# Two experts instead of one get a first part of 256 slots, ahead of the last routing

## The chip, the cores and the metric

The kernel runs on one core of one Trainium2 chip. The metric is device time in microseconds (us) for one launch. In the text PE is the engine for matrix products (TensorE), DVE is VectorE, ACT is ScalarE, POOL is GpSimd, and SP is SyncE, which here only issues transfers. Each of these engines works through a list of its own, in the order of that list. "PEld" is the load of the stationary operand into PE's array.

## The reference, cut to what matters

Three stages follow each other. The first is an attention whose mask lets a query see a key only if both fall in the same of 64 buckets; the second is a dense layer pair with a gated activation; the third is a mixture of eight experts, of which each token takes the best two.

```python
# stage 1: 2 batches, 8 heads, 768 positions, 64 wide
scores = np.where(q_bucket == k_bucket, scale * q @ k.T, -1e9)
x = softmax(scores) @ v                        # -> 1536 tokens x 512
# stage 2
h = x @ w_in                                   # 512 x 2048
x = (h * sigmoid(1.702 * h)) @ w_out           # 2048 x 512
# stage 3: 8 experts, 512 -> 1024 -> 512
noisy = x @ w_gate + log1p(exp(x @ w_noise)) * noise
top2, weights = two largest of noisy per token, softmax over the two
for e in range(8):
    out[mask_e] += weight_e * (relu(x[mask_e] @ w1[e]) @ w2[e])
```

## The kernel before, in words

All products are done in float16 pairs: a value is split into a high and a low half, and three products (high by high, high by low, low by high) stand for one. This goes for the weights too: `w12_split` makes the two halves of a block of expert weights (128x1024), the high one on ACT (L742), the low one on DVE (L743). An expert has eight such blocks, four of w1 and four of w2. They are loaded by `w12_load` on SP into `w32`, of which there are four buffers (`w` in the trace's names), and split into `ew` tiles in the pool `wts`, which has four buffers: two hold one expert's w1 and w2, the other two the next one's. Before the experts the same four hold the weights of stage 2 (`wi` and `wo`).

The 1536 tokens go through stages 1 and 2 in six chunks of 256. A chunk's stage 2 ends with the products `px` (L471), whose two halves of 128 tokens are written to `xr` by ACT (L485) and DVE (L494) and transposed by a DMA to `xrt` (`r_t`). Then `route` works out the two experts of each token. It is written as a generator: products with the gate weights (`pz`, L578 and L580) on PE, a copy on ACT (`zc`, L583), a long run of small operations on DVE with three exponentials on ACT between them (L586 to L645), a count of the tokens ahead of each on PE (`pp`, L650), and a last run on DVE (L655 to L679) that ends with the slot numbers `si`. Four indirect transfers by POOL (L685) then write the chunk's rows to `slots` in DRAM, each to its expert's region of 400 slots.

The experts come after the last chunk. A list `seq` is the order of the steps on PE: a step is either one of the eight slices of an expert's first layer (`l1`, 12 products of the slots' transposed rows `xg` with `ew`, into one of three `ph` tiles in PSUM; ACT, L809, and DVE, L810, empty it into `ht` one step later) or one of the tiles of 128 slots of its second layer (`l2`, `py`), whose result `l2_out` scales on ACT and adds to the output with an indirect transfer by POOL. `e_load` transposes an expert's slots from DRAM to `xg` (L756) and fetches their token numbers and weights (`mt`); `e_meta` makes the scale from these on DVE (L776 to L786).

The last chunk's routing would leave PE idle. So expert 0 is cut in two parts: `reserve` moves its counter up after chunk 4 has been routed, so that the last chunk's tokens stand in slot 256 and above, and slots 0 to 255, the part (0, 0), can be worked on while the last chunk is routed. The part (0, 1) has the other 144 slots. How many experts are cut is `EA`, here 1; the other seven have one part of 400. The last routing is taken apart as `QX` pieces for each step of `seq`.

From step 100 of the program's main loop on, the lists of the engines are as the code emits them. The code is arranged by step numbers: `at(g, f)` puts f behind the rest of step g, `start` and `soon` put it further ahead in it.

```python
w32: x = m2.tile([128, 1024], F32, name="w32", bufs=4)
l1:  ph = psum2.tile([128, CAP], F32, name="ph", bufs=3)
pool of ew, wi, wo: wts = ctx.enter_context(tc.tile_pool(name="wts", bufs=4))
```

Of the kernel before, what the change touches and what calls it, by code (L numbers as in the profile page):

```python
# [52 lines left out]
SW2 = 2.0 ** 6  # L53


PARAM = dict(GM=16, HE=lambda nm, b: 'D', OE=lambda nm, b: 'D', SC=lambda nm, b: 'D', WB=0, XO=lambda b: 'D', NG=16, WS=lambda i: 'P', TS=lambda g: True, XL=lambda g: 'D', GW=2, E0=7, T0=12, T1=16, EL=8, WX=3, PV={(1,2,3):4}, PVD=5, ST={}, VA={}, RA={}, O0=48, OS=2, IS=2, FU=16, VF=2, EC=lambda g: 'AA', QX=8, QS=3, EA=1, S1=(8,8,8,9,9,9,11,13), QE=8, XG=2, XB=2, PC=2, OH=3, BK=3, R0=18, R1=0, LK=8, WL=1, NW=3, LE=lambda nc: nc.scalar, I0=24, LQ=8, LV=0, W=[(g, 1) for g in range(-6, 30)], KA={(0,0,0):-8,(0,0,1):-6,(0,1,0):-4,(0,1,1):-2}, QA={(0,0,0):-7,(0,0,1):-3}, HI=lambda g: 'P', LO=lambda g: False)
# [1095 lines left out]
```

## Time and profile before

| | |
|---|---|
| median of 3 runs | 826.06 us (823.59 to 827.4) |
| the profiled execution | 823.72 us, its span 822.0 us, the rest before its first and after its last instruction |
| PE busy | 715.9 us, 87% of the span |
| DVE busy | 533.9 us, 65% |
| ACT busy | 445.0 us, 54% |
| POOL busy | 267.9 us, 33% |
| DMA | 140.04 MB, mean 170 GB/s |

The span counts from the first to the last instruction. An engine's busy share is an average over the three stages. The experts start some 522 us after the span's start and take the rest of it; PE is busy there with two exceptions.

### The profile page before, as it was taken

To read this page: it belongs to the slowest core of one execution; us is meant where nothing else is said; L and a number is where in the kernel's file an instruction comes from. 1 tells how busy PE (TensorE), PEld (TensorE's weight loads), DVE (VectorE), ACT (ScalarE), POOL (GpSimd) and SP (SyncE) were. 2 spreads that over 40 slices of the span, in tenths; PEclk is the share of its full clock that TensorE was granted. 3 is DMA by queue.
4 is the path that set the end of the run, shared out by engine and by line. 5 is a ranking of instruction groups with operands and counts; after the bars stand their busy time and mean duration, and the time that the engine had idled before them with its cause. 6 is when DMAs were issued, how large, how long until landed. Compare 5 with 4: busy or idle time off the path is not lost.

```text
span 822.0 us, 14816 instructions
## 1 busy us (share of the span) xinstructions
PE 715.9 (87%) x5398; PEld 446.0 (54%) x5399; DVE 533.9 (65%) x1330; ACT 445.0 (54%) x859; POOL 267.9 (33%) x303
## 2 busy tenths in 40 slices
PE   1676478988988888898999999879999999999995
PEld 1343345646754665466568576547554655556553
DVE  8998799997896789569869526454633525345210
ACT  3778767766765686467567425234533534334220
POOL 6444646560444055314212132241021120311212
PEclk9878789999999999999999999999999999999998
DMA  8999689999999999995797542856875858677213
GB/s 218 224 251 212 180 187 184 255 277 218 175 171 195 154 200 192 225 159 106 119 176 123 102 156 88 221 146 180 250 158 173 199 111 232 135 194 176 28 19 47
DMA packets 268126, 140.04 MB, mean 170 GB/s; under 512 B 224720, under 2 KB 243856, under 8 KB 268048
## 3 DMA queue, kind: packets, MB, share of 16 engines
q1 hardware_dynamic: 261520, 125.37, 68.1%
q0 software_dynamic: 6528, 13.68, 9.3%
q8 instruction: 43, 0.70, 0.4%
q14 instruction: 35, 0.29, 0.1%
HBM read 61.48 MB, written 23.79 MB: 104 GB/s over the span
## 4 chain that ended last, share of the span: by engine, by line
PE 42%; DVE 5%; DMA 3%; POOL 2%; issue 1%; ACT 1%; POOLq 0%; ACTq 0%; DVEq 0%
PE ph L799 15%; PE py L821 13%; PE px L471 6%; PE h L460 3%; PE py L825 2%; DVE er L323 1%; DMA xg<-slots 1%; PE pv L368 1%; POOL slots L685 1%; DMA slots<-xr,si 1%; DMA et<-er 1%; PE s L254 1%; ACT er L314 1%; DVE e L266 1%; DVE th L490 1%
## 5 line engine op out<-in xcount | busy, mean ns | idle before, releaser
L460 PE MATMUL h<-xt,wi 128*128 128x256 f16 x1152 | 140.2, 277 | 6.2 <-DVE mx L279 3.2
L799 PE MATMUL ph<-xg,ew 128*128 128x400 f16 (+2 forms) x864 | 135.4, 320 | 8.9 <-DMA xg<-slots 8.4
L743 DVE SCALAR_TENSOR_TENSOR ew<-w,ew 128x1024 f16<-128x1024 f32 x64 | 77.9, 1226 | 88.2 <-ACT ew L742 88.0
L471 PE MATMUL px<-wo,gt 128*128 128x512 f16 x576 | 132.6, 382 | 0.5 <-DVE th L490 0.4
L460 PEld LDWEIGHTS <-wi 128*128 128x128 f16 x1152 | 112.5, 99 | 28.2 <-issue 9.1
L821 PE MATMUL py<-ew,ht 128*128 128x512 f16 x576 | 125.8, 379 | 0.0
L838 POOL DMA_INDIRECT out_dram<-yo,ti x32 | 51.2, 1600 | 216.7 <-ACT yo L835 216.7
L254 PE MATMUL s<-kt,qt 128*128 128x512 f16 (+1 forms) x384 | 88.2, 353 | 33.3 <-DVE mx L266 28.5
L799 PEld LDWEIGHTS <-ew 128*128 128x128 f16 x864 | 82.6, 100 | 59.8 <-issue 6.8
L275 ACT ACTIVATE e<-e,mx 128x768 f32<-128x768 f32 x96 | 89.4, 931 | 27.9 <-DVE mx L266 21.5
L505 POOL TENSOR_TENSOR gt<-th,gt 128x512 f16<-128x512 f32 x48 | 60.1, 1252 | 122.0 <-ACT gt L504 121.6
L266 DVE CUSTOM_DVE_ANT_0 e<-s,zero 128x768 f32<-128x768 f32 x96 | 90.6, 948 | 4.4 <-PE s L254 1.5
L821 PEld LDWEIGHTS <-ht 128*128 128x128 f16 x576 | 56.3, 98 | 67.0
L471 PEld LDWEIGHTS <-gt 128*128 128x128 f16 x576 | 55.3, 98 | 64.1 <-issue 3.2
L323 DVE SCALAR_TENSOR_TENSOR er<-e,mx,er 128x768 f16<-128x768 f32 x68 | 73.1, 1080 | 25.9 <-ACT er L314 25.3
L314 ACT ACTIVATE er<-e,mx 128x768 f16<-128x768 f32 x68 | 63.0, 930 | 37.8 <-DMA et<-er 21.6
L835 ACT ACTIVATE yo<-py,wv 128x512 f32<-128x512 f32 (+1 forms) x32 | 20.3, 633 | 102.4 <-PE py L821 54.6
L809 ACT ACTIVATE ht<-ph 128x400 f16<-128x400 f32 (+2 forms) x72 | 33.5, 466 | 73.0 <-PE ph L799 72.9
L254 PEld LDWEIGHTS <-qt 128*128 128x128 f16 x384 | 37.0, 103 | 62.7 <-issue 38.5
L810 DVE SCALAR_TENSOR_TENSOR ht<-ph,ht 128x400 f16<-128x400 f32 (+2 forms) x72 | 37.6, 524 | 49.5 <-ACT ht L809 49.5
L742 ACT ACTIVATE ew<-w 128x1024 f16<-128x1024 f32 x64 | 66.3, 1047 | 2.6 <-DMA w<-in_moe_w_dram 2.6
L368 PE MATMUL pv<-et,vt 128*64 128x256 f16 x720 | 51.2, 284 | 7.5 <-DMA et<-er 7.5
(195 smaller groups left out, 945.8 us busy)
## 6 DMA issues: line engine op xcount, KB each, us to landing
w<-in_moe_w_dram SPq DMA_DIRECT2D x64, 512.0 KB, 4.6
wraw<-in_moe_w_in_dram SPq DMA_DIRECT2D x16, 512.0 KB, 4.6
wraw<-in_moe_w_out_dram SPq DMA_DIRECT2D x16, 512.0 KB, 4.3
slots<-blank SPq DMA_DIRECT2D x6, 1032.0 KB, 6.8
v<-in_v_dram SPq DMA_DIRECT2D x24, 192.0 KB, 4.1
out_dram<-zeros SPq DMA_DIRECT2D x13, 256.0 KB, 3.4
k<-in_k_dram SPq DMA_DIRECT2D x16, 192.0 KB, 3.6
q<-in_q_dram SPq DMA_DIRECT2D x24, 128.0 KB, 3.1
```

The costliest lines, as they stand in the source:

```text
L254: nc.tensor.matmul(ps[:, n0 * 128:n1 * 128], qt[:, s, h, t, :], kt[:, s, h, n0:n1, :].rearrange("p c t -> p (c t)"), start=(s == 0), stop= ...
L266: nc.vector.tensor_tensor_reduce(e32, st[g]["ps"][:, :S], zero.to_broadcast([128, S]), -0.125, TOP, op0=OP.add, op1=OP.min, accum_out=mx[: ...
L275: nc.scalar.activation(e32, e32, AF.Exp, scale=-1.0, bias=st[g]["mx"][:, 1:2], accum_out=sms[b, cc, hp][:, 2 * h + t:2 * h + t + 1] if g < ...
L314: nc.scalar.activation(er[:, 0], st[g]["e"], AF.Copy, scale=r)
L323: nc.vector.scalar_tensor_tensor(er[:, 1], d["e"], d["mx"][:, 3:4], er[:, 0], op0=OP.mult, op1=OP.subtract)
L460: nc.tensor.matmul(ph[:, a, :], wi[ws][:, d, f0:f0 + 128], xt[:, d, xs, :], start=(d == 0 and ws == 0 and xs == 0), stop=(d == HP - 1 and ...
L471: nc.tensor.matmul(px, gts[ci, f // 2][:, gs, f % 2, t * 128:t * 128 + 128], wo[ws][:, f, :], start=(f == 0 and gs == 0 and ws == 0), stop ...
L505: nc.gpsimd.tensor_tensor(gt[:, 1], th, gt[:, 0], op=OP.subtract)
L742: nc.scalar.activation(hi, x, AF.Copy, scale=SW1 if j == 0 else SW2)
L743: nc.vector.scalar_tensor_tensor(lo, x, SW1 if j == 0 else SW2, hi, op0=OP.mult, op1=OP.subtract)
L799: nc.tensor.matmul(ph[:, :c1 - c0], w[:, ws, d * FE + f * 128:d * FE + f * 128 + 128], xg[e, p][:, xs * HP + d, :], start=(d == 0 and ws = ...
L821: nc.tensor.matmul(py, ht[:, f, hs, t * 128:t * 128 + 128], w[:, ws, f * DM:(f + 1) * DM], start=(i == 0), stop=(i == n - 1))
```

## The change

`EA` goes from 1 to 2: expert 1, too, has a first part of 256 slots and a second of 144, and `reserve` moves up both counters. The order of the parts on PE is now (0,0), (1,0), (0,1), (1,1), then experts 2 to 7 whole. Three things go with it. The routing of chunk 4 (the last but one), which took eight steps and ended behind the first splits of expert 0, is folded into five. The two first parts' slots are loaded one after the other on SP, four steps after that routing's end, behind the loads of expert 0's w2. The last routing gives four pieces a step instead of eight, and its slots are loaded at step 13 instead of 7. Expert 1's splits stand at steps 1, 3, 5, 7, 9, 10, 12 and 14 of `seq`, where five of the eight stood at step 8, the others at 11, 13 and 22; expert 2's are moved to around the part (1, 1).

```diff
-... EA=1, ...
+... EA=2, ...
-... S1=[8, 8, 8, 8, 8, 11, 13, 22], ... QX=8, QS=2, QE=7, ...
+... S1=[1, 3, 5, 7, 9, 10, 12, 14], ... QX=4, QS=2, QE=13, ...
+    def one(gen):
+        next(gen)
...
-            for i in range(1, 4):
-                soon(r0 + i, next, gen)
-                at(r0 + i, piece, gen)
-            at(r0 + 4, piece, gen)
-            start(r0 + 5 + r1, next, gen)
-            at(r0 + 5 + r1, piece, gen)
-            if ci == B * NCH - 2:
-                at(r0 + 6 + r1, done, gen)
-                at(r0 + 6 + r1, reserve)
+            if ci < B * NCH - 2:
...
+            else:
+
+                start(r0 + 1, next, gen)
+                soon(r0 + 1, whole, piece(gen))
+                at(r0 + 1, one, gen)
+                start(r0 + 2, whole, piece(gen))
+                soon(r0 + 2, next, gen)
+                at(r0 + 2, piece, gen)
+                at(r0 + 3, piece, gen)
+                start(r0 + 4, next, gen)
+                at(r0 + 4, piece, gen)
+                at(r0 + 5, done, gen)
+                at(r0 + 5, reserve)
                 for e in range(EA):
-                    at(r0 + PARAM["E0"] + r1, e_load, e, 0)
-                    at(r0 + PARAM["E0"] + 2 + r1, e_meta, e, 0)
+                    at(r0 + 9, e_load, e, 0)
...
+    for e in range(EA):
+        at(3 + 3 * e, e_meta, e, 0)
     for e in range(1, E):
         prev = gs[gs.index((e, 0)) - 1]
-        if e >= EA + 1:
-            b0, b1 = begin[prev], begin[e, 0]
-        else:
-            pass
+        if e >= EA:
+            b0, b1 = begin[prev if e > EA else (0, 1)], begin[e, 0]
         for i in range(8):
-            x = b0 + (b1 - b0) * i // 8 if e >= EA + 1 else PARAM["S1"][i]
+            if e < EA:
+                x = PARAM["S1"][i]
+            elif e > EA:
+                x = b0 + (b1 - b0) * i // 8
+            else:
+                x = b0 + 9 + 2 * i if i < 4 else begin[1, 1] + 2 * (i - 1)
             at(x - PARAM['WX'], w12_load, e, i)
             at(x, w12_split, e, i)
     for e, p in gs[EA:]:
         if p == 1:
-            b0 = PARAM["QE"] + e
-            at(b0, done, gen)
+            b0 = PARAM["QE"] if e == 0 else begin[e, 0] + 8
+            if e == 0:
+                at(b0, done, gen)
             at(b0, e_load, e, p)
-            at(b0 + 1, e_meta, e, p)
+            at(begin[e, p] - 3, e_meta, e, p)
```

DVE, where chunk 4's routing meets the first splits of expert 0 (L743; the `w32` numbers 6315, 6317, 6319, 6321 are its four w1 blocks). Before:

```order
L743 SCALAR_TENSOR_TENSOR ew_6638<-w32_6315,ew_6638 128x1024
L626 CAST ef_6643<-ix_6615 128x4
L630 TENSOR_TENSOR oh_6645<-iota_e_107,ef_6643 128x2x8 x2
L633 TENSOR_TENSOR mk_124<-oh_6645 128x16
L635 TENSOR_TENSOR cum_125<-cum_125,mk_124 128x8
L639 COPY xr_6236<-tok_111 128x2
L642 COPY xr_6236<-ef_6643 128x2
L645 TENSOR_TENSOR d1_6652<-top_6614 128x2
L743 SCALAR_TENSOR_TENSOR ew_6638<-w32_6317,ew_6638 128x1024
L743 SCALAR_TENSOR_TENSOR ew_6638<-w32_6319,ew_6638 128x1024
L743 SCALAR_TENSOR_TENSOR ew_6638<-w32_6321,ew_6638 128x1024
L655 TENSOR_SCALAR d1_6652<-d1_6652 128x2
```

DVE at the same place with the change:

```order
L626 CAST ef_6620<-ix_6584 128x4
L630 TENSOR_TENSOR oh_6622<-iota_e_107,ef_6620 128x2x8 x2
L633 TENSOR_TENSOR mk_124<-oh_6622 128x16
L635 TENSOR_TENSOR cum_125<-cum_125,mk_124 128x8
L639 COPY xr_6236<-tok_111 128x2
L642 COPY xr_6236<-ef_6620 128x2
L645 TENSOR_TENSOR d1_6629<-top_6583 128x2
L490 SCALAR_TENSOR_TENSOR th_6637<-th_6637,h_6592 128x512
L743 SCALAR_TENSOR_TENSOR ew_6655<-w32_6315,ew_6655 128x1024
L655 TENSOR_SCALAR d1_6629<-d1_6629 128x2
```

The last run of the routing (it begins with L655) now stands behind one split instead of four.

SP, from the transposition of the last chunk's first half (`xrt`) to the loads of expert 1's first blocks (`w32` from w1). Before:

```order
L570 DMA_TRANSPOSE xrt_6747<-xr_6731 128x8x128
L756 DMA_TRANSPOSE xg_6785<-slots_127 128x8x256
L761 DMA mt_6787<-slots_127 128x2x8
L570 DMA_TRANSPOSE xrt_6815<-xr_6731 128x8x128
L728 DMA w32_6913<-in_moe2_w1_dram 128x1024
```

SP at the same place with the change:

```order
L570 DMA_TRANSPOSE xrt_6754<-xr_6738 128x8x128
L756 DMA_TRANSPOSE xg_6771<-slots_127 128x8x256
L761 DMA mt_6773<-slots_127 128x2x8
L756 DMA_TRANSPOSE xg_6775<-slots_127 128x8x256
L761 DMA mt_6777<-slots_127 128x2x8
L570 DMA_TRANSPOSE xrt_6811<-xr_6738 128x8x128
L728 DMA w32_6817<-in_moe2_w1_dram 128x1024
```

Expert 1's first slots are new between the first `xg` and the transposition of the last chunk's second half; expert 1's weights stay behind that one.

ACT, from the write of the last chunk's second half (L485) on, where it empties the first slices of the part (0, 0) (L809) and takes the routing's copy and exponentials (L583, L595, L605). Before:

```order
L485 ACTIVATE xr_6731<-px_6734 128x512
L809 ACTIVATE ht_6834<-ph_6821 128x256
L583 ACTIVATE zc_6867<-pz_6850 128x64
L595 ACTIVATE rw_6871<-rw_6871 128x16
L809 ACTIVATE ht_6834<-ph_6837 128x256
L605 ACTIVATE rw_6871<-rw_6871 128x16 x2
L809 ACTIVATE ht_6834<-ph_6879 128x256
L809 ACTIVATE ht_6834<-ph_6900 128x256
L809 ACTIVATE ht_6834<-ph_6934 128x256
```

ACT at the same place with the change:

```order
L485 ACTIVATE xr_6738<-px_6741 128x512
L809 ACTIVATE ht_6836<-ph_6821 128x256
L742 ACTIVATE ew_6852<-w32_6817 128x1024
L583 ACTIVATE zc_6872<-pz_6855 128x64
L809 ACTIVATE ht_6836<-ph_6839 128x256
L595 ACTIVATE rw_6876<-rw_6876 128x16
L809 ACTIVATE ht_6836<-ph_6880 128x256
L742 ACTIVATE ew_6852<-w32_6819 128x1024
L605 ACTIVATE rw_6876<-rw_6876 128x16
L809 ACTIVATE ht_6836<-ph_6901 128x256
```

The splits of expert 1's first blocks (L742) now stand between the emptying of the slices and the steps of the last routing; before they stood behind all of these.

## Rows read from the trace of the kernel before

**Rows 1.** Waits of PE: us in total, times, longest us.

```profile
PE ph L799 <- DMA xg<-slots: 8.4, 2, 4.6
```

**Rows 2.** Timeline of PE: start us, us, instruction and count, idle time before, releaser.

```profile
514.06 7.93 PE L471 MATMUL px<-wo,gt 128*128 128x512 f16 x36
525.76 4.35 PE L799 MATMUL ph<-xg,ew 128*128 128x256 f16 x24 [3.77 <-DMA xg<-slots]
...
530.37 5.40 PE L799 MATMUL ph<-xg,ew 128*128 128x256 f16 x48
...
538.78 10.52 PE L821 MATMUL py<-ew,ht 128*128 128x512 f16 x48
553.92 6.30 PE L799 MATMUL ph<-xg,ew 128*128 128x144 f16 x72 [4.61 <-DMA xg<-slots]
560.77 3.69 PE L799 MATMUL ph<-xg,ew 128*128 128x144 f16 x36 [0.55 <-DVE ht L810]
```

**Rows 3.** Stretches of 2 and 4 us; the column behind POOL's is PE's granted clock.

```profile
528.00:530.00 2.00, 2.00 (x12) 1.40 (x11) 0.43 (x1) 0.00 (x0) 0.00 (x0) 0.50 0.96 381
554.00:558.00 4.00, 4.00 (x40) 4.00 (x40) 2.52 (x12) 1.52 (x3) 0.00 (x0) 0.57 1.16 264
```

**Rows 4.** The chain that ended last, in order of time: start us, us.

```profile
512.93 0.18 DVE si L679
...
517.80 3.79 DMA slots<-xr,si
521.61 4.11 DMA xg<-slots
...
538.35 0.17 DVE si L679
...
549.10 4.78 DMA xg<-slots
...
569.64 2.74 PE py L825 x48
...
607.03 16.35 PE ph L799 x96
```

**Rows 5.** Timeline of DVE around the two routings: start us, us.

```profile
504.95 1.33 DVE L743 SCALAR_TENSOR_TENSOR ew<-w,ew 128x1024 f16<-128x1024 f32 x1 [1.64 <-ACT ew L742]
...
510.23 1.23 DVE L743 SCALAR_TENSOR_TENSOR ew<-w,ew 128x1024 f16<-128x1024 f32 x1 [0.67 <-ACT ew L742]
...
522.65 0.69 DVE L494 SCALAR_TENSOR_TENSOR xr<-px,xr 128x512 f16<-128x512 f32 x1 [3.72 <-ACT xr L485]
...
530.80 0.19 DVE L586 TENSOR_TENSOR z<-zc 128x32 f32<-128x32 f32 x1 [2.37 <-ACT zc L583]
```

**Rows 6.** Groups of instructions, shapes apart, 500 to 620 us: busy us, mean ns.

```profile
L743 DVE SCALAR_TENSOR_TENSOR ew<-w,ew 128x1024 f16<-128x1024 f32 x29 | 35.0, 1227 | 22.0 <-ACT ew L742 21.8
L810 DVE SCALAR_TENSOR_TENSOR ht<-ph,ht 128x256 f16<-128x256 f32 x8 | 3.3, 418 | 1.8 <-ACT ht L809 1.8
```

**Rows 7.** DMA issues 525.6 to 525.8 and 524 to 525.3 us: KB, us to landing.

```profile
w<-in_moe_w_dram SPq DMA_DIRECT2D x1, 512.0 KB, 4.1
xrt<-xr SPq DMA_TRANSPOSE x1, 3.0
```

**Rows 8.** Timeline of SP's queue: start us, us.

```profile
524.36 1.24 SPq L570 DMA_TRANSPOSE xrt<-xr  x1
525.64 2.00 SPq L728 DMA_DIRECT2D w<-in_moe_w_dram  x4
```

**Rows 9.** Timeline of ACT: start us, us, idle time before and releaser.

```profile
545.71 1.06 ACT L742 ACTIVATE ew<-w 128x1024 f16<-128x1024 f32 x1 [2.56 <-DMA w<-in_moe_w_dram]
546.67 0.67 ACT L835 ACTIVATE yo<-py,wv 128x512 f32<-128x512 f32 x1
```

**Rows 10.** PE's weight loads for the first layer, on the page: busy us, mean ns.

```profile
L799 PEld LDWEIGHTS <-ew 128*128 128x128 f16 x864 | 82.6, 100 | 59.8 <-issue 6.8
```

**Rows 11.** First-layer work (tile ph) in one stretch: PE, DVE, ACT busy (count), clock.

```profile
557.50:560.00 2.50, 2.50 (x43) 0.61 (x2) 0.86 (x3) 1.00 1.07 224
```

More of the change, by code (lines that the diff above doesn't have):

```diff
@@ L53 @@
 SW2 = 2.0 ** 6
-PARAM = dict(GM=16, HE=lambda nm, b: 'D', OE=lambda nm, b: 'D', SC=lambda nm, b: 'D', WB=0, XO=lambda b: 'D', NG=16, WS=lambda i: 'P', TS=lambda g: True, XL=lambda g: 'D', GW=2, E0=7, T0=12, T1=16, EL=8, WX=3, PV={(1,2,3):4}, PVD=5, ST={}, VA={}, RA={}, O0=48, OS=2, IS=2, FU=16, VF=2, EC=lambda g: 'AA', QX=8, QS=3, EA=1, S1=(8,8,8,9,9,9,11,13), QE=8, XG=2, XB=2, PC=2, OH=3, BK=3, R0=18, R1=0, LK=8, WL=1, NW=3, LE=lambda nc: nc.scalar, I0=24, LQ=8, LV=0, W=[(g, 1) for g in range(-6, 30)], KA={(0,0,0):-8,(0,0,1):-6,(0,1,0):-4,(0,1,1):-2}, QA={(0,0,0):-7,(0,0,1):-3}, HI=lambda g: 'P', LO=lambda g: False)
@@ new lines @@
+PARAM = dict(GM=16, HE=lambda nm, b: 'D', OE=lambda nm, b: 'D', SC=lambda nm, b: 'D', WB=0, XO=lambda b: 'D', NG=16, WS=lambda i: 'P', TS=lambda g: True, XL=lambda g: 'D', GW=2, E0=7, T0=12, T1=16, EL=8, WX=3, PV={(1,2,3):4}, PVD=5, ST={}, VA={}, RA={}, O0=48, OS=2, IS=2, FU=16, VF=2, EC=lambda g: 'AA', QX=8, QS=3, EA=2, S1=(8,8,8,9,9,9,11,13), QE=8, XG=2, XB=2, PC=2, OH=3, BK=3, R0=18, R1=0, LK=8, WL=1, NW=3, LE=lambda nc: nc.scalar, I0=24, LQ=8, LV=0, W=[(g, 1) for g in range(-6, 30)], KA={(0,0,0):-8,(0,0,1):-6,(0,1,0):-4,(0,1,1):-2}, QA={(0,0,0):-7,(0,0,1):-3}, HI=lambda g: 'P', LO=lambda g: False)
@@ new lines @@
+PARAM.update(KA={(0, 0, 0): -15, (0, 0, 1): -6, (0, 1, 0): -5, (0, 1, 1): -4, (0, 2, 0): -1, (0, 2, 1): 1, (0, 3, 0): 4, (0, 3, 1): 5, (1, 0, 0): 37, (1, 0, 1): 39, (1, 1, 0): 44, (1, 1, 1): 46, (1, 2, 0): 42, (1, 2, 1): 51, (1, 3, 0): 47, (1, 3, 1): 51}, QA={(0, 0, 0): -15, (0, 0, 1): -3, (0, 0, 2): 1, (0, 0, 3): 3, (0, 1, 0): 8, (0, 1, 1): 9, (0, 1, 2): 17, (0, 1, 3): 21, (0, 2, 0): 24, (0, 2, 1): 28, (0, 2, 2): 30, (0, 2, 3): 33, (1, 0, 0): 37, (1, 0, 1): 41, (1, 0, 2): 47, (1, 0, 3): 52, (1, 1, 0): 57, (1, 1, 1): 56, (1, 1, 2): 60, (1, 1, 3): 69, (1, 2, 0): 72, (1, 2, 1): 69, (1, 2, 2): 80, (1, 2, 3): 84}, VA={(0, 0, 0): -1, (0, 0, 1): -3, (0, 1, 0): -1, (0, 1, 1): -1, (0, 2, 0): 0, (0, 2, 1): 0, (0, 3, 0): -1, (0, 3, 1): -2, (1, 0, 0): -1, (1, 0, 1): -1, (1, 1, 0): 2, (1, 1, 1): -4, (1, 2, 0): -3, (1, 2, 1): -3, (1, 3, 0): 2, (1, 3, 1): -2}, PV={(0, 0, 0): 4, (0, 0, 1): 5, (0, 0, 2): 6, (0, 0, 3): 5, (0, 1, 0): 6, (0, 1, 1): 4, (0, 1, 2): 4, (0, 1, 3): 5, (0, 2, 0): 5, (0, 2, 1): 5, (0, 2, 2): 5, (0, 2, 3): 6, (1, 0, 0): 4, (1, 0, 1): 5, (1, 0, 2): 4, (1, 0, 3): 5, (1, 1, 0): 5, (1, 1, 1): 5, (1, 1, 2): 5, (1, 1, 3): 6, (1, 2, 0): 6, (1, 2, 1): 4, (1, 2, 2): 4, (1, 2, 3): 4}, RA={0: 18, 1: 18, 2: 19, 3: 24, 4: 18}, W=[(g,1) for g in [-6, -4, -3, -1, 0, 0, 1, 1, 2, 4, 4, 7, 8, 8, 9, 10, 11, 12, 13, 14, 15, 16, 16, 17, 18, 20, 20, 22, 22, 23, 23, 24]], EC=lambda g:'AA', LE=lambda nc:nc.sync, HI=lambda g:'AAAA'[g%4], LO=lambda g:[0, 0, 0, 1, 0, 0, 0, 1][g%8]==1, S1=[1, 3, 5, 7, 9, 10, 12, 14], ST={0: 4, 1: 4, 2: 5, 3: 4, 4: 5, 5: 3}, NG=28, WS=lambda i:'PAAA'[i%4], HE=lambda nm,b:'DPDD'[2*(nm=='k')+b], OE=lambda nm,b:'DTDD'[2*(nm=='k')+b], SC=lambda nm,b:'DADD'[2*(nm=='k')+b], R1=2, I0=26, IS=1, O0=56, OS=1, GM=100, BK=3, OH=3, QX=4, QS=2, QE=13, VF=0, T0=12, T1=17, EL=10, WX=5, WL=2, PC=2, GW=2, E0=8, WB=2)
@@ L938, in fused @@
             at(r0, piece, gen)
-            for i in range(1, 4):
-                soon(r0 + i, next, gen)
-                at(r0 + i, piece, gen)
-            at(r0 + 4, piece, gen)
-            start(r0 + 5 + r1, next, gen)
-            at(r0 + 5 + r1, piece, gen)
-            if ci == B * NCH - 2:
-                at(r0 + 6 + r1, done, gen)
-                at(r0 + 6 + r1, reserve)
+            if ci < B * NCH - 2:
+                for i in range(1, 4):
+                    soon(r0 + i, next, gen)
+                    at(r0 + i, piece, gen)
+                at(r0 + 4, piece, gen)
+                start(r0 + 5 + r1, next, gen)
+                at(r0 + 5 + r1, piece, gen)
+            else:
[7 more added lines that the diff above has]
+                start(r0 + 4, next, gen)
+                at(r0 + 4, piece, gen)
+                at(r0 + 5, done, gen)
+                at(r0 + 5, reserve)
                 for e in range(EA):
-                    at(r0 + PARAM["E0"] + r1, e_load, e, 0)
-                    at(r0 + PARAM["E0"] + 2 + r1, e_meta, e, 0)
+                    at(r0 + 9, e_load, e, 0)
     for i in range(4):
```

1 line of the change is left out of this document (removed).

## Prediction

> **What bounds the kernel now.** I read the page first, then PE's waits, then PE's, DVE's and ACT's timelines from 500 to 610 us, then the chain of waits in order of time. From the last `px` on, the end is set by PE: the chain is PE alone but for two places. PE has done the last chunk's products at 514.06 + 7.93 = 522.0 us and then waits for `xg`, twice, 8.4 us in all [rows 1]: 3.77 us ahead of part (0,0), 4.61 us ahead of part (0,1), and 0.55 us for an eviction in between [rows 2]. Each of the two long waits is followed by a time at half clock: the granted clock is 0.50 at 528 to 530 us and 0.57 at 554 to 558 us [rows 3], which is 1.2 GHz in place of 2.4. Its price: the first 24 products took 4.35 us, where 24 of the next 48 (5.40 us) took 2.7, so 1.65 us; the 72 narrow ones took 6.30 us, where 72 at 63 ns (below) make 4.5, so some 1.6 us. That makes 3.77 + 1.65 + 4.61 + 0.55 + 1.6 = **12.2 us** that could go. After this the two programs do the same work; the place to compare is 607.03 us [rows 4], where expert 1 is done and the first slice of expert 2 too.
>
> Both waits come from routing. Chunk 4's slot numbers `si` stand at 512.93, the slots are written at 521.61, `xg` takes 4.11 more. The last chunk's `si` stand at 538.35; its `xg` is issued at 549.10 and lands 4.78 later [rows 4].
>
> **The first wait.** DVE does four splits of expert 0 ahead of the last run of chunk 4's routing, from 504.95 to 511.46 [rows 5]. The change leaves one ahead. The run from the fourth split's end to `si` took 1.6 us, so `si` now stands at about 504.95 + 1.33 + 1.7 = 508.0, five us earlier. As before 8.7 us to the written slots and 4.11 to `xg`: 520.8, ahead of 522.0. The loads of w2 that stand before it on SP are issued as the first splits end, by 512, and do not hold it. So 3.77 and 1.65 us go. Folding chunk 4's routing into fewer steps puts `pp` right behind the last `h` and the counting of `reserve` 24 products later; each may wait some tenths for DVE, which I leave at nothing (up to 0.5 us).
>
> **What is late next.** The part (0,0) now starts at 522.0, and 24 products later, at 524.6, PE comes to `pz`, which needs the transposition of the last chunk's second half. DVE writes that half until 523.34 [rows 5] and the transposition lands 3.0 us after its issue [rows 7]: 526.4. Before, the late start covered it. First new wait: 1.8 us.
>
> Expert 1's weights are needed one part earlier, and their loads stand on SP behind that transposition (1.24 us to issue [rows 8]): 524.6, landing 4.1 us on [rows 7], so 528.7. The split of the first block is now second in ACT's list, behind slice 0's eviction. ACT takes its list in order: at 545.71 it idled 2.56 us for such a load, and the eviction behind it waited for the split although its product was done at 544.0 (half of the 10.52 us from 538.78) [rows 2, 9]. So the routing's copy `zc` and slice 1's eviction wait until 529.75 (1.05 us for the split), then on DVE for the low half, 1.23 us [rows 6], two small steps and the `ht` of 0.42 us: 531.8. There are three `ph` tiles, so PE can do slices 2 and 3 (to 529.6) and must wait for slice 1's: second new wait, 2.2 us.
>
> From there to the end of the fourth split DVE has a list without gaps: three splits (3.7 us), five evictions (2.1), 16 routing operations, and 12 of the two `e_meta`. The routing from `z` at 530.80 to `si` at 538.35 holds 39 operations and five evictions: (7.7 - 2.1) / 39 = 0.14 us each, so 28 make 4.0. Sum 9.8: 541.6, and up to 1 us more for exchanges with ACT (three exponentials); I take 542.0. PE does slices 4 to 7 meanwhile and then stands before the first slice of (1,0), which needs all four blocks. Without waits it would be there after 96 products of 112 ns and 0.4 us for `pz`, at 533.1. **So this stretch costs 8.9 us in all.** Its last wait is nearly as long as the two of today, so I add 1.6 us at half clock.
>
> **The second wait.** The (1,0) slice and the second layer of (0,0) (10.5 us) then end at 555.4. `si` of the last chunk now needs slice 1 of (1,0), its eviction and the seventh split ahead of it: 4.4 us, 559.8. From `si` to landed `xg` the trace has 15.5 us for the last chunk and 12.8 for chunk 4 [rows 4], so 572.6 to 575.3. PE has 84 products of 112 ns and 10.5 us to do: 575.3. It is covered, but barely; wait 0 to 0.2 us. The 4.61, 0.55 and 1.6 us go.
>
> **The second cut.** Expert 1's first layer is 96 products of 256 and 96 of 144 columns in place of 96 of 400 (16.35 us, 170 ns each [rows 4]). The narrow ones: 43 fall in 2.5 us at full clock [rows 11], 58 ns; the 36 products in 3.69 us that include 12 wide ones give (3.69 - 2.04) / 24 = 69 ns [rows 2]. I take 63: 96 x (112 + 63 - 170) = 0.5 us, bounds 0 and 1.1. This is where a rule speaks against the change: the Trainium skill, page "TensorE: Matmul & The Clock Gate", section "Back-to-back issue gap", says that in a stream of weight loads and products both set the spacing and that about 81 ns remain at 128 columns. By that the cut would cost 1.7 us more and the sum below would be 1.8 us over the execution's own time; the measured 58 to 69 ns decide against it here.
>
> **Behind it.** In (1,1) the narrow slices (12 x 63 ns = 0.76 us) meet expert 2's splits, one for every two slices: 1.23 us and two evictions of 0.3 on DVE against 1.5 us on PE, so 0.3 us for each of four: 1.3 us. `xg` of (1,1) is issued right behind that of (0,1), a whole part ahead of its use: nothing, or up to 5 us if it fell behind the part. The other loads keep their distance.
>
> **Sum:** -12.2 + 8.9 + 1.6 + 0.5 + 1.3 = **+0.1 us**. The profiled execution took 823.72 us, 2.3 below the median of 826.06; so 826.2. A measurement of this kernel can tell about 0.5%, 4.1 us, from no change: I forecast none.
>
> **Rivals.**
> 1. *Faster: the waits inside (0,0) are short.* The four loads might be there earlier, or the evictions not be held. With the wait for `pz` alone: -12.2 + 1.8 + 0.5 + 1.3 = -8.6, 817.5. With the stretch at 5 us and no half clock: -5.4, 820.7. Against it stands the order of ACT and DVE, which rows 9 show to be kept. It is more than 4.1 us once the fourth split ends before 539.3, with the half clock gone by then.
> 2. *Slower: the gap only moves to (0,1).* The last routing has half the pieces a step, and its last piece now waits for a slice of (1,0) and a split. If `si` or the writes of the slots come 3 us later than I have it, PE waits 3 us and pays 1.6 at half clock: 830.8. It decides from 2.5 us on, that is if `xg` lands after 577.8. For it speaks that cover and need are equal in my sum; against it that 15.5 us is already the longer of two.
> 3. *Narrow products go at the pace of the weight loads.* These last 100 ns each [rows 10]; if they did not overlap, the new narrow part would cost 96 x 37 ns = 3.6 us more: 829.8. Rows 11 speak against it. The Trainium skill's section named above would give 1.7 of these.
> 4. *The change doesn't reach its end at (0,0):* chunk 4's slots are still late, since loads and the first transposition fill the DMA engines then. All of the first wait and its half clock back, less the 1.8 us that it covers: +3.6, 829.8.
>
> **Chances.** Forecast (within 4.1 us): 0.53, which takes in rivals 3 and 4 where they come alone. Rival 1 and all between it and the bound: 0.26. Slower by more: rival 2 0.13, rival 3 or 4 together with another shortfall 0.08. The range for 8 in 10 goes from near rival 1 to beyond rival 2: 818.5 to 831.5.
>
> **What would show it.** PE starts `ph` at about 522 with no wait; a wait of about 2 us at `pz`; waits of `ph` for DVE's `ht`; about 4 us before the first slice of (1,0), released by DVE's `ew`; a granted clock of 0.5 behind it; little or no wait for `xg` at (0,1) near 575; the first slice of expert 2 done near 607. I am wrong if expert 1's fourth block is split well before or after 542, or if (0,1) waits for more than 2 us.

## The result, and the profile after

The changed kernel takes 829.29 us (median of 20 runs, 826.49 to 833.21); the kernel before, run beside it on the same chip, 824.62 us (20 runs). The ratio is 1.0056, 95% between 1.0044 and 1.0069: slower by 4.7 us. The forecast was 826.2 us and no change; the time is inside the range, on its upper side, and the difference is just past the 0.5%, 4.1 us, within which the forecast called it no change.

| | before | after |
|---|---|---|
| the profiled execution | 823.72 us | 830.31 us |
| its span | 822.0 us | 828.6 us |
| PE's waits over 3 us from the last `px` to expert 2 | 3.77, 4.61 | 4.14, 3.25 |
| from the end of `px` to expert 2's second slice | 522.0 to 607.03, 85.0 us | 524.9 to 613.69, 88.8 us |

The page of the profile after, its row of busy time:

```profile
PE 720.1 (87%) x5494; PEld 452.3 (55%) x5495; DVE 536.7 (65%) x1344; ACT 445.7 (54%) x867; POOL 266.6 (32%) x303
```

The waits of PE after, those that lie behind the last `h` (us in total, times, longest us):

```profile
PE ph L799 <- DMA xg<-slots: 4.1, 1, 4.1
...
PE py L821 <- DVE ht L810: 3.2, 1, 3.2
PE ph L799 <- DVE ht L810: 2.1, 4, 0.6
...
PE ph L799 <- DVE ew L743: 1.1, 1, 1.1
...
PE pt L695 <- DVE cum L661: 0.9, 1, 0.9
...
PE pp L650 <- DVE mk L633: 0.5, 1, 0.5
PE ph L799 <- ACT ht L809: 0.5, 1, 0.5
```

They answer to [rows 1]. One of the two waits for `xg` is gone, the one ahead of (0,1); the one ahead of (0,0) is as long as before (4.14 against 3.77). What is new are the waits for DVE, and the longest of these stands at a place that the forecast didn't name: `py`, the second layer.

The timeline of PE after (start us, us, instruction and count, idle time before, releaser), which answers to [rows 2]:

```profile
509.21 15.70 PE L471 MATMUL px<-wo,gt 128*128 128x512 f16 x72
529.05 5.28 PE L799 MATMUL ph<-xg,ew 128*128 128x256 f16 x24 [4.14 <-DMA xg<-slots]
...
534.59 2.78 PE L799 MATMUL ph<-xg,ew 128*128 128x256 f16 x24
537.89 2.78 PE L799 MATMUL ph<-xg,ew 128*128 128x256 f16 x24 [0.52 <-DVE ht L810]
540.94 2.78 PE L799 MATMUL ph<-xg,ew 128*128 128x256 f16 x24 [0.28 <-DVE ht L810]
544.36 1.36 PE L799 MATMUL ph<-xg,ew 128*128 128x256 f16 x11 [0.64 <-DVE ht L810]
546.85 0.28 PE L799 MATMUL ph<-xg,ew 128*128 128x256 f16 x1 [1.13 <-DVE ew L743]
...
574.93 7.26 PE L821 MATMUL py<-ew,ht 128*128 128x512 f16 x25 [3.25 <-DVE ht L810]
582.02 0.91 PE L799 MATMUL ph<-xg,ew 128*128 128x144 f16 x12
...
599.87 3.23 PE L799 MATMUL ph<-xg,ew 128*128 128x144 f16 x48 [0.64 <-DVE ht L810]
603.58 2.19 PE L799 MATMUL ph<-xg,ew 128*128 128x400 f16 x12 [0.49 <-ACT ht L809]
```

`px` ends at 509.21 + 15.70 = 524.9. The 24 products behind the first wait take 5.28 us where the next 24 take 2.78: 2.5 us of half clock. The waits inside (0,0) come to 0.52 + 0.28 + 0.64 + 1.13 = 2.6 us. Ahead of (0,1), at 582.02, PE doesn't wait. The granted clock, behind POOL's column as in [rows 3], shows two stretches at half:

```profile
530.00:532.00 2.00, 2.00 (x12) 1.34 (x11) 0.00 (x0) 0.20 (x1) 0.00 (x0) 0.50 0.88 164
...
576.00:578.00 2.00, 2.00 (x6) 0.76 (x5) 0.00 (x0) 0.04 (x1) 1.65 (x2) 0.50 0.48 107
```

The chain that ended last, after (start us, us), against [rows 4]:

```profile
510.05 0.18 DVE si L679
...
515.47 8.16 DMA slots<-xr,si
523.64 1.86 SPq L756
...
526.17 2.76 SPq L756
...
529.65 1.24 SPq L570
530.93 3.91 DMA w<-in_moe_w_dram
...
545.66 1.14 DVE ew L743
...
566.52 2.76 DMA slots<-xr,si
569.34 1.30 SPq L756
...
571.77 1.66 DMA mt<-slots
...
613.69 16.35 PE ph L799 x96
```

Two things are to be seen. The last write of chunk 4's slots takes 8.16 us, where it took 3.79; and the chain then goes through SP: the transposition of expert 0's first slots and their `mt`, those of expert 1, then the last chunk's `xrt` at 529.65, then expert 1's weights, and the fourth split at 545.66.

At the second place the timeline of DVE shows what the row of `py` can't:

```profile
573.55 0.17 DVE L776 TENSOR_SCALAR wv<-mt 128x2 f32<-128x2 f32 x1 [7.27 <-DMA mt<-slots]
...
574.44 0.42 DVE L810 SCALAR_TENSOR_TENSOR ht<-ph,ht 128x256 f16<-128x256 f32 x1
```

DVE stands idle for 7.27 us for `mt`, the token numbers of (0,1). The instruction that waits is the first of `e_meta` (L776); the last eviction of (1,0) (L810, 0.42 us) is behind it in DVE's list, and `py` needs that eviction. The wait is written down for PE as one for DVE's `ht`; what is late is a DMA.

### The profile page after: what moved, and what is told of

It is laid out like the page before. It is cut to its first block, busy times and chain, and to the rows that moved or that the text cites. A ratio compares the mean times of both kernels' runs of the same rounds, so it can differ in the third digit from the quotient of the medians.

```text
span 828.6 us, 15033 instructions
## 1 busy us (share of the span) xinstructions
PE 720.1 (87%) x5494; PEld 452.3 (55%) x5495; DVE 536.7 (65%) x1344; ACT 445.7 (54%) x867; POOL 266.6 (32%) x303
## 4 chain that ended last, share of the span: by engine, by line
PE 39%; DVE 5%; DMA 4%; ACT 2%; POOL 1%; issue 1%; SPq 1%; POOLq 0%; ACTq 0%; DVEq 0%
PE py L821 14%; PE ph L799 13%; PE px L471 5%; PE h L460 3%; PE py L825 2%; DMA et<-er 2%; DMA slots<-xr,si 1%; PE pv L368 1%; PE s L254 1%; DVE ew L743 1%; POOL slots L685 1%; ACT ew L742 1%; DVE er L323 1%; SPq L756 1%; DVE th L490 1%
## 5 line engine op out<-in xcount | busy, mean ns | idle before, releaser
L460 PE MATMUL h<-xt,wi 128*128 128x256 f16 x1152 | 142.4, 279 | 3.7 <-DVE th L490 2.0
L743 DVE SCALAR_TENSOR_TENSOR ew<-w,ew 128x1024 f16<-128x1024 f32 x64 | 78.2, 1226 | 93.9 <-ACT ew L742 93.9
L821 PE MATMUL py<-ew,ht 128*128 128x512 f16 x576 | 127.9, 383 | 3.2 <-DVE ht L810 3.2
L799 PEld LDWEIGHTS <-ew 128*128 128x128 f16 x960 | 87.6, 99 | 54.6 <-issue 9.3
L810 DVE SCALAR_TENSOR_TENSOR ht<-ph,ht 128x400 f16<-128x400 f32 (+2 forms) x80 | 38.7, 487 | 53.4 <-ACT ht L809 53.2
L809 ACT ACTIVATE ht<-ph 128x400 f16<-128x400 f32 (+2 forms) x80 | 34.7, 436 | 66.6 <-PE ph L799 66.3
L742 ACT ACTIVATE ew<-w 128x1024 f16<-128x1024 f32 x64 | 66.7, 1048 | 6.7 <-DMA w<-in_moe_w_dram 6.7
L368 PE MATMUL pv<-et,vt 128*64 128x256 f16 x720 | 49.1, 275 | 6.9 <-DMA et<-er 6.9
```

Of the source, the lines that this page charges most:

```text
L460: nc.tensor.matmul(ph[:, a, :], wi[ws][:, d, f0:f0 + 128], xt[:, d, xs, :], start=(d == 0 and ws == 0 and xs == 0), stop=(d == HP - 1 and ...
L742: nc.scalar.activation(hi, x, AF.Copy, scale=SW1 if j == 0 else SW2)
L743: nc.vector.scalar_tensor_tensor(lo, x, SW1 if j == 0 else SW2, hi, op0=OP.mult, op1=OP.subtract)
L799: nc.tensor.matmul(ph[:, :c1 - c0], w[:, ws, d * FE + f * 128:d * FE + f * 128 + 128], xg[e, p][:, xs * HP + d, :], start=(d == 0 and ws = ...
L821: nc.tensor.matmul(py, ht[:, f, hs, t * 128:t * 128 + 128], w[:, ws, f * DM:(f + 1) * DM], start=(i == 0), stop=(i == n - 1))
```

## The experiments

Theory: the change loses its gain at two placements, `e_meta` ahead of the last eviction of (1,0), and chunk 4's slots and the last `xrt` behind other transfers (w2's loads, expert 1's slots). The rival: expert 1's weights, which are handed over (loaded and split) during (0,0), are the price, and taking away either of the others only moves the wait to the splits. "Stage" below is the time in the profiled run from the first of the last 96 `px` to expert 2's second slice: 105.9 us before (501.03 to 606.97), 110.65 after (502.97 to 613.62). It leaves out the wait of `pp`, which stands just ahead of it where the routing is folded. "The fourth split's product" is the one that waits for the last of expert 1's four w1 blocks, at 546.85 after: 21.9 us behind the end of `px`.

**1. `e_meta` of the second parts later** (label e1_meta).

```diff
-            at(begin[e, p] - 3, e_meta, e, p)
+            at(begin[e, p] + 2, e_meta, e, p)
```

> Only the scale of each second part (e_meta of (0,1) and (1,1)) is made five steps later. Theory: with the change PE loses 3.25 us and then some 1.8 us at half clock in the second layer of (1,0), because DVE stands at the scale of (0,1), which waits for its token numbers, ahead of the last eviction of (1,0). Then that wait goes, no wait for xg takes its place (it landed near 574 us, PE needs it at 577), and the time falls by 4 to 5 us against the changed kernel, to 1.000 of the kernel before. Rival: the slots themselves are late; then PE waits 2 to 4 us for xg ahead of (0,1) and the time stays at 1.004 to 1.006.

Measured: 823.88 us, ratio 0.9998 (0.9974 to 1.0023), stage 105.1. The timeline of PE:

```profile
567.84 10.52 PE L821 MATMUL py<-ew,ht 128*128 128x512 f16 x48
```

The 48 products of `py` run through, and nothing waits for `xg` at (0,1) either. The one line is worth 0.58% or 4.8 us, what theory said; all of the change's loss to the kernel before. Its first wait was also shorter (2.20) with no half clock behind it, which the edit does not reach. But the waits inside (0,0) were longer (1.66, 2.37 and 0.79), and the fourth split's product stands 21.1 us behind `px`: 0.8 us less. The other 4.8 of the stage's 5.6 us are the edit's.

**2. Two more load buffers** (e2_w6): `w32` gets six, so six of expert 0's eight blocks are loaded early and two instead of four loads run beside the slots' writes.

```diff
-        x = m2.tile([128, 1024], F32, name="w32", bufs=4)
+        x = m2.tile([128, 1024], F32, name="w32", bufs=6)
...
-    for i in range(4):
+    for i in range(6):
...
-        if i < 4:
-            at(NU + 11 + i, w12_load, 0, i + 4)
+        if i < 2:
+            at(NU + 11 + i, w12_load, 0, i + 6)
```

> Six buffers for the raw expert weights instead of four; six of expert 0's eight blocks are loaded early, only two beside the writes of chunk 4's slots. Theory: these writes took 8.2 us to land (3.8 before the change) because all four w2 loads now run beside them; with two the last write lands in 4 to 6 us, PE's first wait for xg falls from 4.1 us to 1 to 2 us, and the time by 2 to 4 us, to 1.001 to 1.004 of before. Rival: the writes are slow by themselves or for the transposition beside them; then they stay near 8 us and the time does not change (1.0056).

Measured: 826.06 us, 1.0012 (0.9994 to 1.0030), stage 108.5. DMA issues (KB each where known, median us to landing), after, from 508 to 516 us:

```profile
w<-in_moe_w_dram SPq DMA_DIRECT2D x4, 512.0 KB, 6.0
slots<-xr,si POOLq DMA_INDIRECT x4, 6.8
xrt<-xr SPq DMA_TRANSPOSE x1, 8.5
```

and in this kernel, from 506 to 515 us:

```profile
slots<-xr,si POOLq DMA_INDIRECT x4, 3.5
```

The same four writes land in 3.5 us in place of 6.8. So the loads beside them were the delay. But the wait came back in two pieces, in the timeline of PE:

```profile
523.93 2.78 PE L799 MATMUL ph<-xg,ew 128*128 128x256 f16 x24 [1.41 <-DVE xr L494]
...
532.46 2.78 PE L799 MATMUL ph<-xg,ew 128*128 128x256 f16 x24 [2.46 <-DVE ht L810]
```

The first products now wait for the emptying of the last `px` (L494), and inside (0,0) there are 2.46 us where there were 0.52. Here the rival is right in part: what is won ahead of (0,0) is partly lost inside it, and the fourth split's product stands 18.9 us behind `px`, 3.1 us less. The stage gains less than that, since the 25 `py` products behind a wait of 3.21 us took longer in this run (8.39 us against 7.26).

**3. Expert 1's first slots behind the last transposition and expert 1's loads on SP** (e3_sp).

```diff
-                for e in range(EA):
-                    at(r0 + 9, e_load, e, 0)
+                at(r0 + 9, e_load, 0, 0)
...
+    at(3, e_load, 1, 0)
```

> The load of expert 1's first slots is issued behind the last chunk's second transposition and expert 1's w1 loads instead of ahead of them. Theory: SP is held up 3.3 us by it (it stands at the late slots, then issues for 2.8 us); without it the transposition and the four loads come 3.3 us earlier, the waits for ht and ew inside (0,0), 2.6 us, fall below 1 us, and the time falls by 1.5 to 2.5 us, to 1.003 to 1.004 of before. Rival: DVE's list in that part is the bound, not the loads; then the waits stay within 0.5 us and the time within 0.1%.

Measured: 825.04 us, 1.0001 (0.9982 to 1.0019), stage 105.4. More than expected: 4.5 us in place of 1.5 to 2.5. `px` ends at 523.36. From the timeline of SP, and from that of PE:

```profile
524.74 1.24 SPq L570 DMA_TRANSPOSE xrt<-xr  x1
```

```profile
541.83 0.28 PE L799 MATMUL ph<-xg,ew 128*128 128x256 f16 x1 [1.12 <-DVE ew L743]
```

`xrt` is issued 1.4 us behind `px`, where it was 4.7 in the changed kernel, and the fourth split's product stands 18.5 us behind it in place of 21.9. These 3.5 us of the stage's 5.3 are the edit's. The rest is that the 25 `py` products behind a wait of 3.29 us ran at full clock (5.57 us against 7.26), and that part isn't the edit's, as far as these rows tell.

**4. The three together** (e4_all).

```diff
-            at(begin[e, p] - 3, e_meta, e, p)
+            at(begin[e, p] + 2, e_meta, e, p)
...
-        x = m2.tile([128, 1024], F32, name="w32", bufs=4)
+        x = m2.tile([128, 1024], F32, name="w32", bufs=6)
...
+    at(3, e_load, 1, 0)
```

> The three edits together. Theory: they remove different waits, so their gains add: 8 to 11 us less than the changed kernel, 0.993 to 0.996 of before. Rival: what is gained at the first wait is given back inside (0,0), where DVE's list (splits, evictions, routing) is as long as forecast, 8 to 9 us of waits; then 0.999 to 1.001.

Measured: 821.05 us, 0.9949 (0.9933 to 0.9965), stage 102.4. The edits are worth 0.58, 0.44 and 0.55% alone and 1.07% together. They don't all add: experiments 2 and 3 reach the same thing in two ways. In both, and here, `xrt` is issued 1.4 us behind `px`, and the fourth split's product stands 18.9, 18.5 and 18.5 us behind it. So 1.07% is about the first edit and one of the other two; what 2 adds to 1 and 3 was not tried. This version is faster than the kernel before.

**5. As 4, with expert 1's four loads of w1 also ahead of the last transposition** (e5_early).

```diff
+                for i in range(4):
+                    at(r0 + 9, w12_load, 1, i)
...
-            at(x - PARAM['WX'], w12_load, e, i)
+            if (e, i) not in [(1, j) for j in range(4)]:
+                at(x - PARAM['WX'], w12_load, e, i)
```

> The three edits together, and expert 1's four w1 loads issued ahead of the last chunk's second transposition, so that they land before part (0,0) starts. Theory: in (0,0) the wait of ht for the first split's load (2.0 us) goes, and the fourth split ends some 4 us earlier; 3 to 4 us less than the three edits, 0.990 to 0.992 of before. Rival: DVE's list alone is as long as PE's work there; then only 0 to 1 us less, 0.994 to 0.995.

Measured: 820.56 us, 0.9953 (0.9932 to 0.9973), stage 103.9: no gain over 4. The timeline of PE says where it went:

```profile
529.53 0.29 PE L578 MATMUL pz<-wg,xrt 128*128 128x32 f16 x4 [3.40 <-DMA xrt<-xr]
```

The transposition now runs beside the loads, and the wait stands at `pz` in place of `ht`.

**6 and 7. The fold of chunk 4's routing by itself.** Once taken out of the changed kernel (e6_nofold: chunk 4 routed as before, slots loaded at its old step), once put alone into the kernel before (e7_fold: the diff's `else` branch without the other edits).

```diff
-            if ci < B * NCH - 2:
...
+            for i in range(1, 4):
+                soon(r0 + i, next, gen)
+                at(r0 + i, piece, gen)
+            at(r0 + 4, piece, gen)
+            start(r0 + 5 + r1, next, gen)
+            at(r0 + 5 + r1, piece, gen)
+            if ci == B * NCH - 2:
+                at(r0 + 6 + r1, done, gen)
+                at(r0 + 6 + r1, reserve)
...
-                    at(r0 + 9, e_load, e, 0)
+                    at(r0 + PARAM["E0"] + r1, e_load, e, 0)
```

This is the first of the two, against the changed kernel; the second, against the kernel before, has the same lines the other way round and the fold's own.

> The changed kernel with chunk 4's routing as it was before the change (eight steps, its last run behind four splits). Theory: the fold costs PE 1.35 us (its products pp and pt wait for DVE) and gains nothing, since the slots' writes it brings forward meet the w2 loads; without it the waits go, the slots land at most 1 us later, and the time is 0 to 2 us less than the changed kernel, 1.003 to 1.006 of before. Rival, as predicted: the fold brings the slots five us forward; then without it PE's first wait is 3 to 5 us longer and the time 1.009 to 1.012 of before.

> The kernel before with only chunk 4's routing folded and its slots loaded a step earlier. Theory: pp and pt wait 1.3 us, the last write of the slots takes 7 to 8 us to land, PE's first wait stays at 3 to 4 us; 0 to 2 us more than before, 1.000 to 1.003. Rival, as predicted: the first wait goes and PE waits 1.8 us at pz; 3 to 4 us less, 0.995 to 0.996.

Measured: without the fold 829.08 us, 1.0047 (1.0027 to 1.0067), stage 109.4, with a first wait of 4.15; the fold alone in before 823.51 us, 0.9981 (0.9963 to 0.9999), stage 105.9, with waits of 2.78 and 4.84 for `xg`. In the changed kernel the fold gains nothing that shows. In before it brings `si` forward, but the last write lands 7.9 us after it is issued, beside the four loads again, so the wait shrinks by 1 us and not by 3.77; `pp` and `pt` wait 0.49 and 0.86 for it.

**8. As 4, without handing over expert 1's w1** (e8_shared). Expert 1's first layer takes expert 0's w1 here, and the four loads and splits are left out, so the time says only what these cost.

```diff
-        w = ew[e, 0]
+        w = ew[0 if e == 1 else e, 0]
...
+            if e == 1 and i < 4:
+                continue
```

> The three edits together, but expert 1's first layer uses expert 0's w1: its four w1 loads and splits are left out, so this says only what they cost. Theory: the waits for ht and ew inside (0,0), 5.3 us with the three edits, fall below 1 us, since DVE then has evictions and routing alone; 4 to 5 us less than the three edits, 0.989 to 0.990 of before. Rival: the last routing's steps hold the evictions up anyway; then 2 us or less, 0.993.

Measured: 817.11 us (4 runs), 0.9897 (0.9870 to 0.9923), stage 98.6. The only wait inside (0,0) is 1.01 us at `pz`. Against 4 that is 0.52%, 4.3 us (by the stages 3.8): what the handing over costs once the placements are mended. The rival's cost is real, and comes on top of the theory's.

**9. As 4, without the fold** (e9_all_nofold).

```diff
-                at(r0 + 5, done, gen)
-                at(r0 + 5, reserve)
...
+                at(r0 + 6 + r1, done, gen)
+                at(r0 + 6 + r1, reserve)
+                at(r0 + PARAM["E0"] + r1, e_load, 0, 0)
```

> The three edits together, but chunk 4's routing as before the change. Theory: the fold is worth something once the w2 loads are out of the way: without it the slots land near 522 us, PE's first wait is 3.5 to 4.5 us with some 1.5 us at half clock behind it, against 1.4 us; pp and pt wait 1.4 us less. So 2 to 4 us more than the three edits, 0.998 to 1.000 of before. Rival: the fold gives nothing here either (as it did on the changed kernel), since the last chunk's second transposition holds PE in any case; then 0.994 to 0.996.

Measured: 820.41 us, 0.9949 (0.9930 to 0.9969), the same ratio as 4. The timeline of PE:

```profile
526.15 4.46 PE L799 MATMUL ph<-xg,ew 128*128 128x256 f16 x24 [4.32 <-DMA xg<-slots]
...
539.23 1.36 PE L799 MATMUL ph<-xg,ew 128*128 128x256 f16 x11 [0.35 <-DVE ht L810]
541.71 0.28 PE L799 MATMUL ph<-xg,ew 128*128 128x256 f16 x1 [1.12 <-DVE ew L743]
```

A first wait of 4.32 us is back, with 1.7 us of half clock behind it (4.46 against 2.78), where 4 waits 1.41: 4.6 us more. Yet the fourth split's product stands only 1.4 us later behind `px` (19.9 us, in 4 18.5): the waits inside are 0.35 in place of 2.01 + 0.27 + 0.64. `pp` and `pt` don't wait, which gives the 1.4 us back (0.48 + 0.89 in 4). So PE's delays in (0,0) aren't added up. What sets the part's end is the other chain, from the last `px` over `xrt`, the loads and the splits. From the issue of `xrt` to the fourth split's product it is 17.1 to 17.5 us in the changed kernel and in experiments 1, 2, 3, 4, 6 and 9 alike, whatever PE waited for before. A wait ahead of the part takes the place of those in it, but for what the late slots, ahead of `xrt` on SP, delay its issue: 2.5 us behind `px` here, 1.4 in 4.

**10. As 4, with the order of PE changed where it met that chain** (e10_nohoist): the first slice of (1,0), which needs all four blocks of expert 1, no longer stands ahead of the second layer of (0,0), and the first six splits come one step later.

```diff
-S1=[1, 3, 5, 7, 9, 10, 12, 14]
+S1=[2, 4, 6, 8, 10, 11, 12, 14]
...
-        if n and (p == 0 or n > EA):
+        if n > 1 and (p == 0 or n > EA):
```

> The three edits together; the first slice of (1,0) is no longer put ahead of the second layer of (0,0), and expert 1's w1 splits stand at steps 2, 4, 6, 8 instead of 1, 3, 5, 7, its first w2 splits at 10, 11, 12, 14. Theory: PE no longer needs the fourth split until 10 us later, and the first split no longer stands ahead of slice 1's eviction; of the 4 to 5 us that expert 1's weights cost in (0,0) with the three edits, 2.5 to 4 go: 0.990 to 0.992 of before. Rival: the evictions still meet the splits in DVE's list and PE waits for ht as long as now: 0.994 to 0.995.

Measured: 818.86 us, 0.9925 (0.9895 to 0.9955), stage 100.1. The timeline of PE:

```profile
534.48 2.78 PE L799 MATMUL ph<-xg,ew 128*128 128x256 f16 x24 [0.83 <-DVE ht L810]
537.55 1.47 PE L799 MATMUL ph<-xg,ew 128*128 128x256 f16 x12 [0.30 <-DVE ht L810]
538.86 10.52 PE L821 MATMUL py<-ew,ht 128*128 128x512 f16 x48
```

Eight slices of (0,0), and then its second layer without a wait: the fourth split has 10.5 us more. The stage is 2.3 us shorter than in 4; by the ratios 10 is 0.24% ahead of 4, and the two intervals overlap.

**11. One cut expert, with the fold and six buffers** (e11_one: the kernel before, with experiments 2 and 7 put in).

```diff
-        x = m2.tile([128, 1024], F32, name="w32", bufs=4)
+        x = m2.tile([128, 1024], F32, name="w32", bufs=6)
...
+            if ci < B * NCH - 2:
...
+            else:
...
+                at(r0 + 5, done, gen)
+                at(r0 + 5, reserve)
...
-    for i in range(4):
+    for i in range(6):
```

The edit is against the kernel before, so `EA` stays at 1.

> One expert with a first part, as before the change, with chunk 4's routing folded and six buffers for the raw weights. Theory: the first wait and its half clock go but for 1.4 to 2 us; the second wait (4.6 us, 1.6 at half clock) stays, which only the second cut can cover: 2 to 4 us less than before, 0.995 to 0.998, 0 to 2 us above the three edits. Rival: the second cut gives nothing; then this is as fast as or faster than the three edits, 0.993 to 0.995.

Measured: 822.06 us, 0.9959 (0.9939 to 0.9979), stage 102.6, with 4.00 us for the second `xg` still there. So most of what 4 has over before doesn't need the second cut; by the ratios the cut adds 0.1% in 4, inside the intervals, and 0.34% in 10, where its hand-over is mended; there, too, the intervals overlap. So a gain of the second cut by itself is likely, and not shown.

**12. As 10, the fold's last two steps one step later** (e12_late), so that `pp` and `pt` find their data.

```diff
-                start(r0 + 4, next, gen)
-                at(r0 + 4, piece, gen)
-                at(r0 + 5, done, gen)
-                at(r0 + 5, reserve)
+                at(r0 + 4, one, gen)
+                at(r0 + 5, piece, gen)
+                at(r0 + 6, done, gen)
+                at(r0 + 6, reserve)
```

> The kernel without the hoist, and the last two steps of chunk 4's folded routing one step later. Theory: pp and pt (0.5 and 0.9 us of waits since the fold) find their inputs ready, and the slots, which then land some 1.5 us later, still come before PE can start (0,0), which has 3 us in hand there; 1 to 1.4 us less than without the edit, 0.989 to 0.992 of before. Rival: the later slots show as a wait of ph for xg, and the time does not change or is longer: 0.993 or more.

Measured: 816.93 us, 0.9922 (0.9891 to 0.9953). The waits of `pp` and `pt` are gone, the first wait is 2.44 in place of 1.41; by the time it can't be told from 10. Both beat the two kernels by 6 us and more.

## Why the prediction was right and where it was wrong

The time fell into the range. The point was 3.1 us short in time, and 4.6 us in the difference (+0.1 forecast, 4.7 measured; the median that the forecast started from was 1.4 us above that of the 20 runs). Two terms were put at nothing, and a third that was too dear made up for much of it. By the chances the result is among the cases "Slower by more", which had 0.21. By the steps of the sum, in us, with the rows above (the half clock at `py` is 7.26 less the 5.57 that the same 25 products took at full clock in experiment 3):

| term | forecast | measured |
|---|---|---|
| both waits of before, eviction, half clock | -12.2 | -12.2 |
| first wait left, half clock behind it | 0 | 4.14 + 2.5 |
| waits inside (0,0), to the fourth split | 8.9 | 2.6 |
| half clock behind the fourth split | 1.6 | 0 |
| `pp` and `pt` for DVE | 0 | 0.49 + 0.86 |
| from (1,0) to (0,1): `py`, half clock | 0 | 3.25 + 1.7 |
| second cut, narrow products | 0.5 | 0.4 |
| (1,1) beside expert 2's splits | 1.3 | 0.64 + 0.49 |
| sum | +0.1 | +4.9 |

The sum of the right column stands against 4.7 us by the ratio. The two profiled spans are 6.6 us apart; PE reaches the `pz` ahead of this stage at 490.15 in one and 491.22 in the other, and this 1.1 us isn't the change's (in the experiments the same `pz` stands anywhere between 488.05 and 493.28).

- **The first wait** was to go, and did not. The step that failed is "as before 8.7 us to the written slots", with the clause that the loads of w2 "do not hold it". `si` came as forecast: 14.9 us ahead of the end of `px`, forecast 14.0. But from `si` to the written slots it took 13.6 us. The 8.7 had been read in a stretch where the loads were nearly over; bringing `si` forward put the writes among them. This is rival 4, and experiment 2 shows the cause. `xg` then took 5.4 us (523.64 to 529.05) in place of 4.11; with as many loads and the same second transposition behind it, it took 4.1 in experiment 6, so the cause of these 1.3 us stays open.
- **The stretch of (0,0)** was rightly seen and slightly too dear: 4.14 + 2.5 + 2.6 = 9.2 us against 8.9 + 1.6. The forecast had no first wait and long ones inside; the run had it the other way round. Experiment 9 shows why the make-up matters little: the chain over `xrt`, the loads and the splits sets the end. That step of the forecast held, the fourth split ending at 546.80, 21.9 us behind `px`, forecast 20.0. Inside it two errors met: `xrt` was issued 3.4 us later than forecast (4.7 us behind `px` in place of 1.3), and from there to the split's end it took 17.2 us in place of 18.7. What SP did for expert 1's slots ahead of `xrt` (526.17 to 529.65) stood in SP's order as it was read, and wasn't priced; experiment 3 shows that it counts.
- **The second wait** was forecast by the landing of `xg`, and that was right: no wait at (0,1). The step that failed is "wait 0 to 0.2 us", since it followed only PE's need of `xg`. `e_meta` needs the same late slots and is in DVE's list three steps earlier. The gap moved as rival 2 has it, though through DVE's list, at another line and without `xg` being late. Experiment 1 shows it, and that this term alone is as large as the whole loss.
- **`pp` and `pt`** were to be left "at nothing (up to 0.5 us)"; it was 1.35 us in all.
- **The second cut** is right. From the chain after:

```profile
582.94 6.02 PE ph L799 x96
```

  96 narrow products in 6.02 us are 63 ns each, as taken; the wide ones took 111 ns (84 in 9.33 us), so 96 x (111 + 63 - 170) = 0.4 us. Rival 3 didn't happen, and the 81 ns of the Trainium skill (page "TensorE: Matmul & The Clock Gate", section "Back-to-back issue gap") are not what this stream shows.
- **(1,1)**: 1.1 us against 1.3.

That the error stayed below 5 us has one piece of luck in it: the first wait, missed with 6.6 us, took the place of waits that had been charged at 10.5.

## What to carry to other kernels

A small operation that waits for a DMA blocks all that is behind it on its engine's list; when routing is made later, follow each reader of its result on each engine, not only the matrix product that needs it most. A transfer's time read in a quiet stretch is not its time in the stretch to which a change moves it: look at what the queues carry there. And where two chains end at the same product, a wait removed from the one comes back inside the other, so price the later of the two ends and not the sum of the waits.

## What the runs showed of the hardware that was not expected

- The four indirect writes of POOL took 6.8 us (median; the last 8.16) beside four loads of 512 KB, 3.5 us where two of the loads had been taken away, and 4.6 us in the kernel before; the transposition `xrt` beside them took 8.5 us, against 5.1 for the same one before and the 3.0 of [rows 7].
- A small DVE operation can last seven times its usual time beside one of POOL. From the timelines of POOL and DVE after:

```profile
502.85 1.20 POOL L505 TENSOR_TENSOR gt<-th,gt 128x512 f16<-128x512 f32 x1 [2.17 <-ACT gt L504]
```

```profile
502.95 1.12 DVE L645 TENSOR_TENSOR d<-top 128x2 f32<-128x2 f32 x1
```

  Two columns take 1.12 us, where they take 0.15 in experiment 3, and end when POOL does; L607 and L615 do the same at 496.85 (1.12) and 499.53 (1.18), where L607 elsewhere takes 0.17. This agrees with the Trainium skill, page "SBUF — State Buffer", section "SBUF: two separate sides": DVE and GpSimd have a pair of ports in common which one instruction holds for all of its time. L607 and L615 lie on the way to `mk`, for which `pp` waits, and L645 on the way to `si`. The kept traces show that L615 makes that wait: in experiments 2 and 3 it took 0.17 and 0.18 us, POOL's operation beginning with it took 1.20 and 1.21, and `pp` didn't wait; after, and in experiments 1, 4, 5, 7, 8, 10 and 11, it took 1.18 and `pp` waited 0.48 or 0.49 us.
- The first product of the experts waited 1.41 us for the emptying of the last `px` (L494) in each run whose slots were there in time (experiments 2, 4, 5, 8, 10 and 11). In the kernel before the longer wait for `xg` covered it, and no run here starts with less.
- Behind a wait of 3.2 to 3.3 us at `py` the same 25 products took 7.26 us (after), 8.39 (experiment 2) and 5.57 (experiments 3 and 6). The granted clock was 0.50 at 576 to 578 us after and at 571 to 575 in experiment 2, and 1.00 throughout in 3 and 6: the half clock behind a wait of one length isn't the same in each execution, and a term for it has an error of up to some 2 us.
